# Causal attention with a soft mixture of experts: v loaded head by head

## Chip, cores and metric

The kernel runs on one core of one Trainium2 chip. The metric is the device time of one execution in microseconds (us). A profile of one execution, taken on the same kernel, gives the time of every instruction and DMA packet.

## What is computed

Attention over 8 batches and 8 heads, 576 queries, 16 "beacon" keys ahead of 576 causal ones, head size 64, all in float32; then a soft mixture of 8 experts with 4 slots each over the 4608 tokens of width 512.

```
k_all = concat([beacon_k, k]); v_all = concat([beacon_v, v])        # (B, H, 592, 64)
scores = q @ k_all.T / sqrt(64); causal mask past the beacons
a = softmax(scores)
x = (a @ v_all) laid out as (4608, 512)
logits = x @ phi                                                     # (4608, 32)
slot_input = softmax over tokens (logits).T @ x                      # (32, 512)
slot_out[e] = relu(slot_input[e] @ w1[e]) @ w2[e]                    # w1 (512, 1024), w2 (1024, 512)
out = softmax over slots (logits) @ slot_out                         # (4608, 512)
```

v has the shape (8, 8, 576, 64): the rows of one batch and one head lie in one piece, 64 float32 (256 B) a row, and the next head begins 147 KB further on.

## The kernel before

The kernel works through 32 pairs of heads, four pairs to a batch (the loop of line 571; n is the pair, b its batch, g its place in the batch). In each turn of the loop the program interleaves, in an order written out by hand for all engines (`manual_schedule`, line 531):

- `scores` (line 416): TensorE (PE) multiplies k and q in four pieces (L422), ScalarE (ACT) takes the exponential out of PSUM (L426), GpSimd (POOL) sets the masked part to zero (L434).
- `transposes` (line 395) of the next pair's q and k on PE (L404), copied out by VectorE (DVE; L409, L413).
- `attend` (line 439): PE multiplies the exponentials of the pair before by v (L448); `normalize` divides on DVE (L459 to L462).
- `x_transposes`, `logits`, `dispatch` and `combine_T` for a batch that is done.
- `cast_v` (line 360): POOL turns v of the next batch from float32 into float16, in five chunks of up to 128 rows. Chunks 0 to 2 are cast at the end of the first pair of a batch, chunks 3 and 4 at the end of the second. The 16 beacon rows are the first rows of chunk 0.
- `load_weights(2)` (line 380): POOL asks for two chunks of expert weights, 256 KB each as float16 (the transfer casts from float32), on a DMA queue of POOL's own, q0 in the profile.

The transfers of q, k, v and the beacons are asked for by SyncE (SP), on queue q1 in the profile. Their order on SP is that of the program. In the steady part, in the second pair of batch b, it asks for the first half of k and q of batch b+2 (L346), then for v of batch b+2 (the beacon rows, L352, then the five chunks, L356); in the fourth pair for the second half of k and q of batch b+2. So a round on SP is: two halves of k and q, four transfers of 576 KB; the beacon rows, 32 KB; five transfers of v, 224, 256, 256, 256 and 160 KB.

q and k have buffers for four halves each (pool `stq`, line 327). The float32 stage of v, `vstag`, has one buffer (pool `stv`, line 328, `bufs=1`): v of a batch can only be asked for when the last cast of the batch before it is done. The float16 copies, `vh`, are two.

The scheduler gives each transfer that SP asks for one of eight completion counters, in turn. A transfer therefore waits, on SP, until the transfer eight places before it on that queue has landed.

At the start SP asks for four transfers of k and q, eight for the beacon keys (32 KB each, L535), v of batch 0, two transfers of k and q, the router matrix phi (64 KB), two of k and q, v of batch 1 and two of k and q. After the last pair the experts are computed (L648 and following), and the output is written in 12 transfers (L717). A fallback path (`general_path`) for extreme inputs is not taken.

Of the kernel before, what the change touches and what calls it, by code (L numbers as in the profile page):

```python
# [268 lines left out]
def kernel(  # L269
# [12 lines left out]
    nc = tc.nc  # L282
    P = 128
    B, H, S, D = q.shape
# [51 lines left out]
    def head(g, hh):  # L336

        return 4 * (g // 2) + 2 * hh + g % 2
# [11 lines left out]
    def load_v(b):  # L350
        t = st["v", b] = stv.tile([P, NC5, H, D], FP, name="vstag", tag="v")
        nc.sync.dma_start(out=t[0:Nb, 0, :, :], in_=beacon_v[b].rearrange("h p d -> p h d"))  # L352
        lo = 0
        for c in range(NC5):
            p0, p1 = (Nb if c == 0 else 0), KW[c]
            nc.sync.dma_start(out=t[p0:p1, c, :, :],  # L356
                              in_=v[b, :, lo:lo + p1 - p0, :].rearrange("h p d -> p h d"))
            lo += p1 - p0

    def cast_v(b, c):  # L360
# [170 lines left out]
    with tc.manual_schedule(engines={ET.PE, ET.DVE, ET.Activation, ET.Pool, ET.SP}):  # L531
        bkf = stv.tile([P, H, D], FP, name="bkf", tag="bkf")
        load_qk(0, 0, first=True)
        for b in range(B):
            nc.sync.dma_start(out=bkf[Nb * b:Nb * b + Nb, :, :],  # L535
                              in_=beacon_k[b].rearrange("h n d -> n h d"))
        load_v(0)
        load_qk(0, 1)
        phif = work.tile([P, NDC, NSL], FP, name="phif", tag="phif", bufs=1)
        nc.sync.dma_start(out=phif[:, :, :], in_=moe_phi.rearrange("(c p) e -> p c e", p=P))  # L540
        load_qk(1, 0)
        load_v(1)
        load_qk(1, 1)

# [13 lines left out]
        for g in range(NG):  # L558
            nc.vector.tensor_copy(
                out=bkh[:, g, :, :],  # L560
                in_=bkf[:, head(g, 0):head(g, 1) + 1:2, :].bitcast(BF)[:, :, 1::2])
# [9 lines left out]
        for n in range(NPAIR + 4):  # L571
            b, g = divmod(n, NG)
# [30 lines left out]
            if live:  # L603
                if b + 1 < B and g < 2:
                    for c in ((0, 1, 2), (3, 4))[g]:
                        cast_v(b + 1, c)
                if g == 1 and b + 2 < B:
                    load_qk(b + 2, 0)
                    load_v(b + 2)
                if g == 3 and b + 2 < B:  # L610
                    load_qk(b + 2, 1)
                if n == NPAIR - 1:
                    siz = work.tile([P, NDC, E * (NSL + SPE)], F16, name="siz", tag="vc", bufs=1)
                    nc.gpsimd.memset(siz[:, :, :], 0.0)
                load_weights(2)
# [7 lines left out]
            out=siz[:, :, :].rearrange("p t (e w) -> p t e w", w=NSL + SPE)[:, :, :, 0:SPE],  # L623
# [56 lines left out]
        for src, w, low in ((stat, NST + 36 + NSL, SUM_LO), (so1, Dm, -SUM_HI)):  # L680
            lo = gd.tile([P, w], FP, name="lo", tag=f"lo{w}")
# [73 lines left out]
```

## Time and profile before

| what | us |
|---|---|
| median of three runs | 253.48 (251.63, 253.48, 261.88) |
| the profiled execution | 249.34 |
| its span, first to last instruction | 247.6 |
| busy: PE, DVE, ACT, POOL | 179.4, 125.2, 128.1, 121.7 |
| mean TensorE clock granted | 0.84 of full speed |
| issues of L356, 40 transfers of v: least, median, most | 0.424, 2.488, 7.911 |
| from an issue of a whole chunk of v (256 KB) to its landing, median | 11.0 |

How to read the profile: an engine's busy time is the time in its instructions. DMA share is the mean busy share of the core's 16 DMA engines; q0 is the queue of the weights, q1 that of everything SP asks for. The chain is followed back from the last instruction, at each step to what released it; "SPq L356" in it is SP issuing a transfer of line 356, "DMA vstag<-in_v_dram" is such a transfer under way. An issue on SP takes long where it waits for a counter or where the queue is full.

### The profile page before, as it was taken

The page shows a single profiled execution, that of the slowest core. Times are in us where ns is not written, and L with a number is a line of the kernel's source. Part 1 is how long each engine was busy: PE and PEld are TensorE (multiplying, and loading weights), DVE is VectorE, ACT ScalarE, POOL GpSimd, SP SyncE. Part 2 cuts the span into 40 slices and gives each one's busy share as a digit, 9 for nine tenths or more (in the row PEclk, how much of TensorE's full clock was granted, in tenths as well). Part 3 has the DMA queues.
Part 4 walks back from the last instruction along what each step waited for, and adds up shares of the span by engine and source line. Part 5 has one row for each costly group of instructions (what it writes and reads, how often), then busy time and mean ns, then how long its engine had stood idle before and what let it go on. Part 6 is the DMA issues. An engine that isn't in the chain of part 4 may idle for free.

```text
span 247.6 us, 8090 instructions
## 1 busy us (share of the span) xinstructions
PE 179.4 (72%) x3469; PEld 125.8 (51%) x3469; DVE 125.2 (51%) x277; ACT 128.1 (52%) x175; POOL 121.7 (49%) x256
## 2 busy tenths in 40 slices
PE   0345799849887987998699788749989697964350
PEld 0223466536665764766467566536766572531110
DVE  0305455705674586556348756535565630256650
ACT  2053547725674566568466677535689212055440
POOL 3042785296459365844945595187467500092000
PEclk9999999975996599589759999775899955999555
DMA  6699999999999999999999999999667720049993
GB/s 209 129 286 282 258 309 219 189 296 273 228 219 326 242 228 283 287 214 228 322 253 225 227 289 238 224 268 208 106 106 124 123 43 0 3 182 416 413 388 143
DMA packets 60061, 55.73 MB, mean 225 GB/s; under 512 B 42096, under 2 KB 42096, under 8 KB 60016
## 3 DMA queue, kind: packets, MB, share of 16 engines
q1 hardware_dynamic: 50800, 38.35, 53.0%
q0 software_dynamic: 9216, 16.78, 37.4%
q8 instruction: 29, 0.48, 0.7%
q14 instruction: 16, 0.13, 0.2%
HBM read 62.46 MB, written 9.44 MB: 290 GB/s over the span
## 4 chain that ended last, share of the span: by engine, by line
DMA 37%; PE 20%; POOL 13%; SPq 12%; DVE 8%; ACT 4%; issue 3%; DVEq 0%; POOLq 0%; ACTq 0%
DMA vstag<-in_v_dram 28%; SPq L356 11%; DMA out_dram<-osb 6%; PE av L448 5%; POOL vh L361 5%; POOL expT L434 5%; PE sc L422 4%; PE hps L648 3%; DVE x L462 2%; DMA qstag<-in_q_dram 2%; PE rsps L662 2%; ACT expT L426 2%; ACT osb L710 2%; DVE kT L413 1%; PE trps L404 1%
## 5 line engine op out<-in xcount | busy, mean ns | idle before, releaser
L426 ACT ACTIVATE expT<-sc 128x992 f16<-128x992 f32 (+3 forms) x128 | 107.1, 864 | 77.7 <-PE sc L422 75.6
L434 POOL TENSOR_SCALAR_AFFINE_SELECT expT<-expT 128x224 f16<-128x224 f16 (+3 forms) x128 | 54.3, 445 | 50.5 <-ACT expT L426 49.7
L448 PE MATMUL av<-vh,expT 128*128 128x65 f16 (+1 forms) x960 | 52.4, 214 | 14.3 <-POOL expT L434 12.6
L422 PE MATMUL sc<-qT,kT 64*128 64x80 bf16 (+4 forms) x576 | 52.3, 279 | 8.2 <-DVE qT L409 6.1
L448 PEld LDWEIGHTS <-expT 128*128 128x128 f16 (+1 forms) x960 | 41.5, 110 | 31.1 <-POOL expT L434 18.0
L361 POOL CAST vh<-vstag 128x512 f16<-128x512 f32 (+1 forms) x40 | 23.9, 614 | 29.8 <-DMA vstag<-in_v_dram 24.0
L459 DVE TENSOR_SCALAR stat<-av 128x10 f32<-128x10 f32 x32 | 5.4, 169 | 60.5 <-PE av L448 60.5
L413 DVE COPY kT<-trps 128x576 bf16<-128x576 bf16 x32 | 24.1, 752 | 7.9 <-PE trps L404 7.8
L422 PEld LDWEIGHTS <-kT 64*128 64x128 bf16 x576 | 18.2, 102 | 17.9 <-DVE qT L409 5.4
L462 DVE TENSOR_TENSOR x<-av,r 128x640 f16<-128x640 f32 x32 | 26.4, 825 | 1.1
L409 DVE COPY qT<-trps 128x576 bf16<-128x576 bf16 x32 | 23.9, 746 | 0.0
L475 PE MATMUL xtps<-idh,x 128*128 128x128 f16 (+2 forms) x160 | 15.4, 237 | 8.7 <-DVE kT L413 7.3
L710 ACT ACTIVATE osb<-fps,rc 128x512 f32<-128x512 f32 x18 | 11.6, 688 | 15.8 <-PE fps L707 11.2
L404 PE MATMUL trps<-idb,qstag 64*64 64x64 bf16 x576 | 17.0, 207 | 3.0 <-DVE xT L479 2.8
L404 PEld LDWEIGHTS <-kstag 64*64 64x64 bf16 x576 | 13.7, 122 | 9.1 <-issue 8.9
L404 PE MATMUL trps<-idb,kstag 64*64 64x64 bf16 x576 | 17.6, 210 | 0.0
L404 PEld LDWEIGHTS <-qstag 64*64 64x64 bf16 x576 | 15.0, 123 | 3.7 <-issue 3.7
L713 DVE TENSOR_SCALAR osb<-fps,rc 128x512 f32<-128x512 f32 x18 | 12.9, 748 | 7.7 <-DMA out_dram<-osb 5.3
L475 PEld LDWEIGHTS <-x 128*128 128x128 f16 (+2 forms) x160 | 11.4, 107 | 10.6 <-issue 6.9
L707 PE MATMUL fps<-so,eT 128*128 128x512 f16 x36 | 11.8, 442 | 5.6 <-ACT osb L710 4.5
L479 DVE COPY xT<-xtps 128x576 f16<-128x576 f16 x32 | 14.3, 449 | 1.4 <-PE xtps L475 1.0
L386 POOL DMA_DIRECT2D w1h<-in_moe_w_dram x24 | 13.2, 553 | 0.0
(68 smaller groups left out, 141.0 us busy)
## 6 DMA issues: line engine op xcount, KB each, us to landing
out_dram<-osb SPq DMA_DIRECT2D x12, 768.0 KB, 4.2
kstag<-in_k_dram SPq DMA_DIRECT2D x15, 576.0 KB, 7.9
qstag<-in_q_dram SPq DMA_DIRECT2D x15, 576.0 KB, 7.5
vstag<-in_v_dram SPq DMA_DIRECT2D x24, 256.0 KB, 11.0
w1h<-in_moe_w_dram POOLq DMA_DIRECT2D x24, 256.0 KB, 8.5
w2h<-in_moe_w_dram POOLq DMA_DIRECT2D x24, 256.0 KB, 8.8
wt<-in_moe_w_dram POOLq DMA_DIRECT2D x16, 256.0 KB, 4.9
vstag<-in_v_dram SPq DMA_DIRECT2D x8, 224.0 KB, 13.1
```

The costliest lines, as they stand in the source:

```text
L356: nc.sync.dma_start(out=t[p0:p1, c, :, :], in_=v[b, :, lo:lo + p1 - p0, :].rearrange("h p d -> p h d"))
L361: nc.gpsimd.tensor_copy(out=vhs[b % 2][0:KW[c], c, :, 0:D], in_=st["v", b][0:KW[c], c, :, :])
L404: nc.tensor.transpose(tp[64 * hh:64 * hh + 64, j, :], hi, idb[lo:lo + 64, lo:lo + 64])
L409: nc.vector.tensor_copy(out=qTs[n][:, :].rearrange("p (s j) -> p s j", j=NJ), in_=src)
L413: nc.vector.tensor_copy(out=kT[:, Nb:Nb + S].rearrange("p (s j) -> p s j", j=NJ), in_=src)
L422: nc.tensor.matmul(sc[:, hh, col:col + qw], kTs[n % 2][po:po + D, c * P:(c + 1) * P], qTs[n][po:po + D, q0:q0 + qw], start=True, stop=True)
L426: nc.scalar.activation(ex[:, :, base:base + w], sc[:, :, 0:w], AF.Exp, scale=scale)
L434: nc.gpsimd.affine_select(out=ap, in_=ap, compare_op=AL.is_ge, fill=0.0, base=cbase, pattern=pat, channel_multiplier=-1)
L448: nc.tensor.matmul(av[:, i, :], exps[n % 2][0:KW[c], hh, o:o + P], vhs[b % 2][0:KW[c], c, h, :], start=(c == 0), stop=(c == i))
L462: nc.vector.tensor_tensor(out=xs[b][:, :, head(g, 0):head(g, 1) + 1:2, :].rearrange("p i h d -> p h i d"), in0=av[:, :, :, 0:D], in1=r[:, ...
L475: nc.tensor.transpose(tp[:, QLO[i]:QLO[i] + QW[i]], xs[b][0:QW[i], i, 2 * t:2 * t + 2, :].rearrange("p h d -> p (h d)"), idh[0:QW[i], 0:QW ...
L710: nc.scalar.activation(osb[:, j - j0, :], fp_[:, :], AF.Copy, scale=rc[:, bb, j:j + 1])
```

## The change

In `load_v`, each of the five chunks of a batch is asked for in eight transfers, one per head, in place of one for all heads. A transfer then has 112, 128 or 80 rows of 256 B that lie in one piece in DRAM (28, 32 or 20 KB), and puts one 256 B row into each partition. The 40 transfers of v become 320. The beacon rows, the casts and the order of all other instructions are as before; each cast waits for the eight transfers of its chunk.

```
@@ -353,8 +353,8 @@
         lo = 0
         for c in range(NC5):
             p0, p1 = (Nb if c == 0 else 0), KW[c]
-            nc.sync.dma_start(out=t[p0:p1, c, :, :],
-                              in_=v[b, :, lo:lo + p1 - p0, :].rearrange("h p d -> p h d"))
+            for h in range(H):
+                nc.sync.dma_start(out=t[p0:p1, c, h, :], in_=v[b, h, lo:lo + p1 - p0, :])
             lo += p1 - p0
```

More of the change, by code (lines that the diff above doesn't have):

```diff
@@ L355, in load_v @@
             p0, p1 = (Nb if c == 0 else 0), KW[c]
-            nc.sync.dma_start(out=t[p0:p1, c, :, :],
-                              in_=v[b, :, lo:lo + p1 - p0, :].rearrange("h p d -> p h d"))
+            for h in range(H):
+                nc.sync.dma_start(out=t[p0:p1, c, h, :], in_=v[b, h, lo:lo + p1 - p0, :])
             lo += p1 - p0
```

## Prediction

> **What bounds the kernel now**
>
> I read the page first (shares, slices, queues), then the chain of waits in order of time, the waits of POOL, the DMA queue's own timeline on SP, and last the DMA view of short windows.
>
> The page:
>
> ```profile
> span 247.6 us, 8090 instructions
> ...
> DMA  6699999999999999999999999999667720049993
> ...
> DMA packets 60061, 55.73 MB, mean 225 GB/s; under 512 B 42096, under 2 KB 42096, under 8 KB 60016
> ## 3 DMA queue, kind: packets, MB, share of 16 engines
> q1 hardware_dynamic: 50800, 38.35, 53.0%
> q0 software_dynamic: 9216, 16.78, 37.4%
> ...
> DMA 37%; PE 20%; POOL 13%; SPq 12%; DVE 8%; ACT 4%; issue 3%; DVEq 0%; POOLq 0%; ACTq 0%
> DMA vstag<-in_v_dram 28%; SPq L356 11%; DMA out_dram<-osb 6%; PE av L448 5%; POOL vh L361 5%; POOL expT L434 5%; PE sc L422 4%; PE hps L648 3%; DVE x L462 2%; DMA qstag<-in_q_dram 2%; PE rsps L662 2%; ACT expT L426 2%; ACT osb L710 2%; DVE kT L413 1%; PE trps L404 1%
> ```
>
> See: no engine passes 72%, the DMA engines are full from about 12 to 173 us, and the largest item of the chain is the transfer of v. Most packets are under 512 B: those of v are 256 B rows, and 8 x 576 x 8 = 36864 of the 42096 are theirs.
>
> One batch in the chain (start, length, what), and how long POOL's casts wait for v (total, times, longest):
>
> ```profile
> 50.65 0.62 POOL vh L361
> 51.27 1.02 POOL w1h L386 x2
> 52.29 1.62 POOL expT L434 x4
> 53.91 1.13 POOL vh L361 x2
> ...
> 55.05 0.33 SPq L352
> ...
> 55.43 0.42 SPq L356
> ...
> 55.90 5.62 SPq L356
> ...
> 61.57 11.58 DMA vstag<-in_v_dram
> ```
> ```profile
> POOL vh L361 <- DMA vstag<-in_v_dram: 24.0, 12, 5.5
> ```
>
> See: vstag has one buffer. The last two casts of a batch free it, SP then asks for the next batch's v, its third chunk lands at 73.2 us, and the casts follow. The beacon transfers of line 352 that open a round stand at 32.27, 55.05, 77.67, 100.30, 122.41 and 144.58 us: a round takes 22.5 us.
>
> Price of an issue on SP, and of small transfers (timeline of SP; then the line view of L535 with the fewest, median and most ns, and its landing times):
>
> ```profile
> 2.67 2.80 SPq L535 DMA_DIRECT2D bkf<-in_beacon_k_dram  x6
> ```
> ```profile
> L535 SPq DMA_DIRECT2D bkf<-in_beacon_k_dram x8: 311/430/432, 2.7 to 7.7; - x8
> ...
> DMA to landing us min/median/max: 1.7/4.1/5.2
> ```
>
> See: transfers of 32 KB, the size that v gets, issued back to back, take 0.43 us each and start 0.475 us apart.
>
> The two queues together, from 63 to 65 us (v and weights), and the first queue with q and k almost alone, 52.5 to 54.5 us:
>
> ```profile
> q0 software_dynamic: 201, 0.35, 93.3%
> q1 hardware_dynamic: 200, 0.06, 19.7%
> ```
> ```profile
> q1 hardware_dynamic: 375, 0.77, 100.9%
> ```
>
> See: where weights (q0) and v (q1) meet, they go packet for packet, 201 to 200, although a weight packet is 2 KB (0.933 x 32 us / 171 = 0.175 us) and one of v 0.031 us. So v crawls beside weights. Alone, q and k move at 0.77 MB / 2 us = 385 GB/s.
>
> **The change, part by part**
>
> **Bytes and packets of v: nothing gained.** A row of v still lands as 256 B in its partition, so the 36864 packets stay. That one transfer now lies in one piece in DRAM could only help if pieces were joined; the first four k and q transfers also lie in one piece, and their packets are still 2304 B rows. Even a gain would hide behind the issue, below: the eight packets per engine of a 32 KB transfer take 8 x 18 ns = 0.15 us (q1 from 70.5 to 72.5 us, v without weights: 1615 packets in 92.3% of 32 us), against 0.475 us to issue it. 280 more transfers add 280 x 16 completion writes, 9 ns each in the packet records: 2.5 us per engine over the run, hidden in the same way. The casts on POOL wait for eight counters in place of one or two; only the last cast of a round is on the path, some 0.1 us each, 1 us in all and left out.
>
> **Issues: 320 in place of 40.** The duration is not in the trace for the new shape (128 rows of 256 B). Bounds: 0.37 us apart (the beacon issue of 0.33 us, plus the 0.045 us gap) and 0.66 us (the eight issues of L535 over 5.29 us, waits included). I take 0.475 us, the back-to-back rows of the same 32 KB. A batch of v then costs SP 40 x 0.475 = 19 us; today its first batch took 4.22 us. On SP alone a round would be 45 issues, 21.4 us, just under 22.5.
>
> **But they don't run beside q and k.** In both builds each SP transfer takes one of eight completion counters in turn, and is held until the transfer eight before has landed. A round on SP is: four transfers of k and q, the beacon rows, 40 of v. After q and k only three of v go freely; the fourth to seventh wait for q and k to land one by one, the eighth for the beacon rows. So the stream of v really starts when the last q has landed. The round becomes a sum:
> - four transfers of k and q: 4 x 0.59 MB / 385 GB/s = 6.1 us;
> - start and landing round them: 1.7 us, the shortest landing of L535;
> - the remaining 33 of v and the next k: 34 x 0.475 = 16.2 us;
> - weights: two chunks per pair, eight per round, 2.10 MB at 0.35 MB / (0.933 x 2 us) = 188 GB/s, 11.2 us of all engines. Bounds: 0 (all between issues that SP makes anyway: beside an idle ring v needs only 0.15 of its 0.475 us) and 11.2 (nothing moves in q1 meanwhile). Beside q and k they add nearly in full: the four transfers took from 51.5 to 64.5 us in place of 6.1. Beside v, eight transfers in flight keep SP going 8 x 0.475 = 3.8 us, more than one burst of two chunks (2.8 us alone), but not two in a row. I take half, 5.6.
>
> Sum 29.6 us, against 22.5. Compute needs no more than today's round, so it waits: behind a cast that waits on POOL stand the weight transfers and the masks (L434) of the next pair, for which PE's products with v (L448) wait; behind v on SP stand q and k, asked for a batch ahead, which do not come late.
>
> **The start.** SP reaches the first v at 8.48 us, ends its 40 issues at 27.5 (12.7 today). The first casts, which ended at 19.2 us, end near 30. Then four transfers of q and k and the router matrix (6.1 + 0.4 + 1.7 us) hold the counters to 35.7; 34 issues to 51.9; landing 1.7 and cast 0.6: the second batch is cast at 54.2 us, against 32.3. So +21.9.
>
> **The rounds.** Six more batches of v, five rounds of 29.6 and a last one with only two of q and k (26.6): 54.2 + 148 + 26.6 = 228.8 us. Today the last cast ends at 167.7. From there on nothing differs; the tail of 80 us stays. So +61.1 us, and 249.3 (the profiled execution; span 247.6 and 1.7 around it) gives 310.4. The median shown is 253.5, 1.7% above that execution; I keep to the execution.
>
> **Rivals**
>
> *Weights stop v altogether.* For: 200 against 201 packets; a 32 KB transfer beside weights needs 8 x (0.175 + 0.031) = 1.65 us, so the eight in flight last long. Against: bursts are 2.8 us with pauses. At the full 11.2 us a round is 35.2: 54.2 + 176 + 32.2 = 262.4, 344 us in all. Half the weights with 0.66 us an issue gives a round of 35.8 and 361.
>
> *Cheap issue, or weights hidden.* At 0.37 us a round is 26.0 and the second batch is cast at 46.4: 46.4 + 130 + 23 = 199.4, so 281 us. With 0.475 and weights at nothing: round 24.0, 54.2 + 120 + 21 = 195.2, so 277. For it: the 0.33 us of a lone beacon issue. Against: back to back no row shows it.
>
> *Not slower: the issue follows the size of a transfer.* If an issue cost SP in proportion to its packets, 128 in place of 1024, 0.42 us would become 0.05, SP would be done in 2 us, and only the ring would count, with the same bytes: a round of 22.5 and about 250 us. It decides from an issue under some 0.26 us, where start and rounds give back the 61 us. Against: L535, with 128 packets, costs 0.43 us, a whole chunk of v 0.42. The Trainium skill (DMA: Bandwidth & Descriptors, Issuing engines are not separate DMA queues) says that the sequencer's time to initiate a DMA is usually small relative to the DMA itself; by it this rival would hold, with 250 us. The rows disagree at this size: 0.475 us to issue what the ring moves in 0.15, which gives 310.
>
> *The one piece is read as one.* If it were, v at the 385 GB/s of q and k in place of 229 (70.5 to 72.5 us) would spare 2.1 us a round, 15 us in all and 235 us; but only with the rival before it, and no packet supports it.
>
> **How the numbers follow**
>
> Forecast, a round of 27.5 to 32.5 us (298 to 328 us): 0.62. Cheap issue or hidden weights (277 to 298): 0.18. Weights in full (328 to 361): 0.13, above that 0.02. Not slower: 0.04, and faster 0.01. The likeliest is 310 us. The range 281 to 344 takes the ends of the two unknown costs and leaves out the not-slower cases, the lowest of the second and the upper half of the third, under 0.2 together. 2%, about 5 us, is what a measurement of this kernel can tell from no change: faster 0.01, same 0.04, slower 0.95.
>
> **What would show it**
>
> Issue: the line of v on SP with 320 instructions near 0.43 us where it doesn't wait. Rounds: the beacon issues of line 352 some 30 us apart, the third of them near 54 us. Serial order: in a round, q and k packets first, then v at 60 to 70 GB/s (32 KB per 0.475 us) with the DMA share well under full. Chain: SP's issue of v as the largest item. POOL's waits for v should grow from 24 us to some 80. Wrong if the issues are under 0.3 us apart, if v flows while q and k are under way, or if compute rather than v ends the rounds.

## The result, and the profile after

The changed kernel takes 342.8 us (median of four runs, 339.8 to 343.8) against 252.6 us: a ratio of 1.359, 95% interval 1.345 to 1.373. The forecast was 310 us in a range of 281 to 344. The direction held, and the mechanism in the main; the size is 1.2 us under the upper end of the range. The profiled execution took 342.68 us, with a span of 341.0.

From the page after:

```profile
span 341.0 us, 8508 instructions
...
DMA  5226528965795579558955795379737968302995
...
DMA packets 64544, 55.78 MB, mean 164 GB/s; under 512 B 46576, under 2 KB 46576, under 8 KB 64496
## 3 DMA queue, kind: packets, MB, share of 16 engines
q1 hardware_dynamic: 55280, 38.36, 37.7%
q0 software_dynamic: 9216, 16.78, 28.9%
...
DMA 41%; SPq 24%; PE 16%; POOL 5%; DVE 4%; issue 4%; ACT 2%; DVEq 0%; POOLq 0%; ACTq 0%
DMA vstag<-in_v_dram 30%; SPq L357 23%; PE av L448 4%; DMA out_dram<-osb 4%; DMA qstag<-in_q_dram 3%; PE sc L422 3%; DMA kstag<-in_k_dram 3%; POOL expT L434 2%; DMA vstag<-in_beacon_v_dram 2%; PE hps L648 2%; PE lgps L486 2%; PE trps L404 1%; PE rsps L662 1%; DVE x L462 1%; DVE osb L713 1%
```

See three things. The row of DMA slices, solid nines before, now swings between 3 and 9 in the rounds: the engines wait for requests. The packets under 512 B rose by 46576 - 42096 = 4480, which is 280 x 16 completion writes and nothing else; the rows of v are still 36864 packets of 256 B. And SP's queue, 12% of the chain before, is 24%; SP's issue of v alone is 23%, second to the transfers of v with 30%.

The line view of the changed line (fewest, median and most ns of an issue; then landing), and SP's waits (total, times, longest):

```profile
L357 SPq DMA_DIRECT2D vstag<-in_v_dram x320: 312/430/1491, 8.6 to 259.6; - x160
...
DMA to landing us min/median/max: 1.6/2.2/15.1
```
```profile
SPq L357 <- DMA vstag<-in_v_dram: 28.9, 31, 2.6
SPq L357 <- DMA qstag<-in_q_dram: 26.4, 12, 4.6
SPq L357 <- DMA kstag<-in_k_dram: 13.1, 8, 3.5
SPq L357 <- DMA vstag<-in_beacon_v_dram: 6.9, 6, 1.3
```

See: an issue costs the 0.43 us that the beacon keys showed before. Where SP does not issue v, it waits for a completion counter: 75.3 us in all, more than half of it for k, q and the beacon rows.

One round on SP, and a piece of the chain in it (start, length, what):

```profile
90.64 0.34 SPq L352 DMA_DIRECT2D vstag<-in_beacon_v_dram  x1
91.03 30.50 SPq L357 DMA_DIRECT2D vstag<-in_v_dram  x40
...
124.95 0.34 SPq L352 DMA_DIRECT2D vstag<-in_beacon_v_dram  x1
```
```profile
92.66 14.28 DMA vstag<-in_v_dram
...
106.96 0.33 SPq L357
...
107.33 0.43 SPq L357
...
113.02 1.77 DMA vstag<-in_v_dram
```

See: 40 issues last 30.5 us. The first few stand in the queue behind k and q and then crawl beside the weights, until 107 us; from there on SP issues without a break until 119.6 us, where the last two wait for v transfers that crawl beside the next weights. The beacon issues stand at 59.30, 90.64, 124.95, 158.34, 193.14 and 229.18 us, 34.0 us apart (22.5 before).

The queues in both states, from 99 to 103 us, then from 108 to 114 us:

```profile
q0 software_dynamic: 387, 0.71, 94.1%
q1 hardware_dynamic: 387, 0.11, 18.8%
```
```profile
DMA packets 1851, 0.42 MB, mean 70 GB/s; under 512 B 1851, under 2 KB 1851, under 8 KB 1851
```

See: beside weights, as many packets of v as of weights, as before. Without them v moves at 70 GB/s, 32 KB per 0.475 us, and its engines are busy 31.8% of the time: the pace is SP's.

Where the 93.4 us of span went: the second batch is cast at 59.3 us in place of 32.2 (+27.1); from there to the last cast, 203.1 us in place of 135.5 (+67.6); the rest takes 78.6 in place of 79.9 (-1.3).

### The profile page after: what moved, and what is told of

Read it like the earlier page. It is cut to its first block, busy times and chain, and to the rows that moved or that the text cites. A ratio compares the mean times of both kernels' runs of the same rounds, so it can differ in the third digit from the quotient of the medians.

```text
span 341.0 us, 8508 instructions
## 1 busy us (share of the span) xinstructions
PE 198.4 (58%) x3469; PEld 136.7 (40%) x3469; DVE 124.4 (36%) x277; ACT 128.6 (38%) x175; POOL 122.1 (36%) x256
## 2 busy tenths in 40 slices
DMA packets 64544, 55.78 MB, mean 164 GB/s; under 512 B 46576, under 2 KB 46576, under 8 KB 64496
## 4 chain that ended last, share of the span: by engine, by line
DMA 41%; SPq 24%; PE 16%; POOL 5%; DVE 4%; issue 4%; ACT 2%; DVEq 0%; POOLq 0%; ACTq 0%
DMA vstag<-in_v_dram 30%; SPq L357 23%; PE av L448 4%; DMA out_dram<-osb 4%; DMA qstag<-in_q_dram 3%; PE sc L422 3%; DMA kstag<-in_k_dram 3%; POOL expT L434 2%; DMA vstag<-in_beacon_v_dram 2%; PE hps L648 2%; PE lgps L486 2%; PE trps L404 1%; PE rsps L662 1%; DVE x L462 1%; DVE osb L713 1%
## 5 line engine op out<-in xcount | busy, mean ns | idle before, releaser
L448 PE MATMUL av<-vh,expT 128*128 128x65 f16 (+1 forms) x960 | 60.4, 225 | 78.2 <-POOL expT L434 77.3
L448 PEld LDWEIGHTS <-expT 128*128 128x128 f16 (+1 forms) x960 | 46.6, 117 | 99.8 <-POOL expT L434 87.8
L361 POOL CAST vh<-vstag 128x512 f16<-128x512 f32 (+1 forms) x40 | 24.6, 614 | 129.7 <-DMA vstag<-in_v_dram 126.3
L422 PE MATMUL sc<-qT,kT 64*128 64x80 bf16 (+4 forms) x576 | 56.5, 302 | 21.8 <-DVE qT L409 20.3
L422 PEld LDWEIGHTS <-kT 64*128 64x128 bf16 x576 | 18.9, 108 | 32.3 <-DVE qT L409 19.6
L413 DVE COPY kT<-trps 128x576 bf16<-128x576 bf16 x32 | 24.1, 754 | 11.2 <-PE trps L404 11.1
L409 DVE COPY qT<-trps 128x576 bf16<-128x576 bf16 x32 | 23.9, 747 | 0.0
L475 PE MATMUL xtps<-idh,x 128*128 128x128 f16 (+2 forms) x160 | 17.0, 254 | 8.6 <-DVE kT L413 7.2
L404 PE MATMUL trps<-idb,qstag 64*64 64x64 bf16 x576 | 18.2, 215 | 2.5 <-DVE xT L479 2.4
L404 PEld LDWEIGHTS <-kstag 64*64 64x64 bf16 x576 | 14.8, 130 | 10.6 <-issue 7.0
L404 PE MATMUL trps<-idb,kstag 64*64 64x64 bf16 x576 | 18.7, 218 | 0.0
L404 PEld LDWEIGHTS <-qstag 64*64 64x64 bf16 x576 | 16.1, 131 | 3.1 <-issue 3.1
L475 PEld LDWEIGHTS <-x 128*128 128x128 f16 (+2 forms) x160 | 12.5, 115 | 10.8 <-issue 6.6
L707 PE MATMUL fps<-so,eT 128*128 128x512 f16 x36 | 13.0, 490 | 4.9 <-ACT osb L710 4.0
```

The costliest lines, as they stand in the source:

```text
L361: nc.gpsimd.tensor_copy(out=vhs[b % 2][0:KW[c], c, :, 0:D], in_=st["v", b][0:KW[c], c, :, :])
L404: nc.tensor.transpose(tp[64 * hh:64 * hh + 64, j, :], hi, idb[lo:lo + 64, lo:lo + 64])
L409: nc.vector.tensor_copy(out=qTs[n][:, :].rearrange("p (s j) -> p s j", j=NJ), in_=src)
L413: nc.vector.tensor_copy(out=kT[:, Nb:Nb + S].rearrange("p (s j) -> p s j", j=NJ), in_=src)
L422: nc.tensor.matmul(sc[:, hh, col:col + qw], kTs[n % 2][po:po + D, c * P:(c + 1) * P], qTs[n][po:po + D, q0:q0 + qw], start=True, stop=True)
L448: nc.tensor.matmul(av[:, i, :], exps[n % 2][0:KW[c], hh, o:o + P], vhs[b % 2][0:KW[c], c, h, :], start=(c == 0), stop=(c == i))
```

## Experiments

Times are device us; each batch ran beside the kernel before on the same chip (251.5, 252.2 and 252.0 us). Rounds are the distances of the beacon issues in the steady part. Runs given without an interval are single ones.

### Few weights, in the changed kernel and in the kernel before

```
-    wchunks = [(e, m, j) for es_ in ((0, 1, 2, 3), (4, 5)) for m in range(2)
-               for e in es_ for j in range(4)]
-    tail = [(e, m, j) for m in range(2) for e in (6, 7) for j in range(4)]
-    wchunks += tail
+    wchunks = [(e, m, j) for m in range(2) for e in (0, 1) for j in range(4)]
+    tail = []
...
     def weight(e, m, j):
...
+        e = e % 2
```

> The changed kernel with 16 of the 64 weight transfers: experts 2 to 7 use the weights of experts 0 and 1 (that part of the computation is left out). The weights then move in the first eight pairs alone, and the last four rounds have none. Theory (issues on SP and the eight completion counters set the round; the weights' time on the shared engines comes on top nearly in full): a round with weights stays near 32 to 34 us, one without falls to the sum of the other terms, 6.1 + 1.7 + 16.2 = 24.0 us; about 295 us in all. Rival (weights slow v only where SP would have waited anyway; the extra 4 us a round over the forecast come from the small transfers themselves): rounds stay at 30 us or more, total 320 to 340 us.

> The kernel before, with the same 16 of 64 weight transfers (experts 2 to 7 use the weights of experts 0 and 1). If the full DMA engines set its round of 22.5 us, rounds without weights fall to what compute needs, some 18 to 20 us, and the total to 230 to 240 us. If compute set it, the total stays at 249 us within 2%.

Measured: 316.7 us for the changed kernel, 229.7 for the kernel before. A round of the changed kernel in which no weight moves:

```profile
152.94 0.34 SPq L352 DMA_DIRECT2D vstag<-in_beacon_v_dram  x1
153.33 25.25 SPq L357 DMA_DIRECT2D vstag<-in_v_dram  x40
...
181.29 0.51 SPq L352 DMA_DIRECT2D vstag<-in_beacon_v_dram  x1
```

Such rounds last 28.7 us (124.32 to 210.49 in three), against 34.0 with weights: the weights cost 5.3 us a round, not their full 11.2. So the first theory was wrong in saying "nearly in full", and also in its 24.0 us for the rest; the total lies just under the 320 to 340 us of the rival, which had put the excess outside the weights. What is missing there shows in the DMA slices of this kernel from 151 to 162 us (0.275 us each), in which SP gets no more than the first eight of v issued:

```profile
DMA  1179559999999999999999999999720140030003
...
q8 instruction: 2, 0.03, 1.4%
```

The first k is asked for at 150.6 us, but the engines move at their full rate only from 152.7 on. The packets of k and q fill them to about 159 us, and the last q transfer lands at 160.8: the number of 2304 B packets per us falls from 166 (157 to 158 us) to 41, 7 and 1. A transfer has landed when its last completion write has come. Of the sixteen of this q, fifteen had come by 159.1 us; the last one came 1.6 us later. The eighth v transfer is issued 10.5 us after the first k, where the forecast had 7.8. In the four rounds of k, q and v without weights these are 10.0, 10.5, 11.2 and 10.6 us, though the late last write stands out in two of them only.

Two of the 33 issues from the eighth v on last 1.3 and 1.4 us without a wait that the profile names, 1.9 us more than their share. From its first k to the next this round takes 10.5 + 33 x 0.475 + 1.9 = 28.1 us; the forecast's 24.0 has 7.8, one issue more and no long ones.

In the kernel before, rounds without weights fall from 22.5 to 17.8 us (96.73 to 132.30 in two): there the full engines had set the round.

### Issue alone

The same few weights, and no k and q transfers after the first two batches.

```
-        t = st["kq"[which], b, hb]
+        t = st["kq"[which], b % 2, hb]
...
-                    load_qk(b + 2, 0)
                     load_v(b + 2)
-                if g == 3 and b + 2 < B:
-                    load_qk(b + 2, 1)
```

> The changed kernel with 16 of the 64 weight transfers (experts 2 to 7 use the weights of experts 0 and 1) and without the k and q transfers of batches 2 to 7 (they use k and q of batches 0 and 1); both parts of the computation are left out. In the later rounds SP then asks for v and the beacon rows alone, on engines that are nearly idle. Theory (the price of an issue on SP is the floor): round 40 x 0.475 = 19.0 + 0.4 for the beacon rows + 3.5 from the last issue to its landing, the cast and the next beacon issue = 22.9 us, as long as a whole round of the kernel before; about 280 us in all, against 316.7 with k and q. Rival (the issues hide; what costs is waiting on k, q and weights): rounds of 18 us or less, as compute had them in the kernel before with few weights, and about 255 us.

Measured: 289.0 us; the late rounds are 24.6 us (111.97 to 185.88 in three).

```profile
160.78 0.32 SPq L352 DMA_DIRECT2D vstag<-in_beacon_v_dram  x1
161.15 22.53 SPq L357 DMA_DIRECT2D vstag<-in_v_dram  x40
185.88 0.32 SPq L352 DMA_DIRECT2D vstag<-in_beacon_v_dram  x1
```

With the engines nearly idle, a round with v alone takes longer than a whole round of the kernel before (22.5 us). The 40 issues are 20.9 to 22.5 us of it; landing, cast and the next beacon issue are the rest. The theory's floor stands; it was 1.7 us too low, since it had 19 us for the issues.

### Tiny extra transfers, v not divided

The kernel before, with seven transfers of 2 KB behind each of v's 40.

```
+    dum = stv.tile([Nb, 7, D // 2], FP, name="dum", tag="dum")
...
+            for i in range(7):
+                nc.sync.dma_start(out=dum[:, i, :], in_=beacon_v[b, i, :, 0:D // 2])
```

> The kernel before, v in 40 transfers of all heads, and after each of them seven transfers of 2 KB (16 rows of 128 B) to a scratch tile that nobody reads: as many issues on SP and as many completion counters taken as in the changed kernel, but v not divided. Theory (issues and counters): rounds of 31 to 35 us, total 325 to 345 us. Rival (the division of v itself costs, by its pieces on the engines): about 250 to 260 us.

Measured: 360.5 us, rounds of 36.5 (95.16 to 241.02 in four). As many requests with hardly a byte in the extra ones cost more than the change; a 2 KB transfer also takes 0.42 us to issue in the median. The number of requests is enough for a loss of this size; the division of v's data is not needed for it. But the round is not made in quite the same way: in each steady round one issue, that of the first extra transfer behind k, q, the beacon rows and a whole chunk, lasts 9.1 to 10.1 us without a wait that the profile names, where the changed kernel waits for counters. Each chunk also waits for the chunk before it, eight places ahead, but only 8.5 us in the whole run. What makes the excess over the changed kernel was not tried apart.

### Two and four heads per transfer

```
-            for h in range(H):
-                nc.sync.dma_start(out=t[p0:p1, c, h, :], in_=v[b, h, lo:lo + p1 - p0, :])
+            for h in range(0, H, 2):
+                nc.sync.dma_start(out=t[p0:p1, c, h:h + 2, :],
+                                  in_=v[b, h:h + 2, lo:lo + p1 - p0, :].rearrange("h p d -> p h d"))
```

and the same with 4 for 2.

> v asked for in 160 transfers of two heads each. Theory (number of issues on SP, and the eight counters): round 6.1 + 1.7 + 14 x 0.475 + about 10 of weights = 24.5 us, second batch cast near 41 us, 41 + 5 x 24.5 + 21.5 = 185 against 167.7: about 266 us. Rival (cost grows evenly from 40 to 320 transfers): 40 to 320 gave +91 us, so 160 gives +39, 288 us. Rival (the loss is in transfers that lie in one piece of one head): back at 250 us.

> v asked for in 80 transfers of four heads each. Theory (issues and counters cost only what exceeds the engines' time): ten issues a round, 11.9 for k, q and beacon rows to land + 4 x 0.475 + 5.5 of weights = 19.3 us, under the 22.5 that the engines need, so as the kernel before: 246 to 258 us. Rival (the cost grows evenly with the number of transfers, 91 us for 280 more): 265 us.

| transfers of v | us (median) | ratio to before, 95% interval | round, us |
|---|---|---|---|
| 40 | 252.0 | | 22.5 |
| 80 | 257.9 | 1.020 (1.012 to 1.028) | 23.6 |
| 160 | 277.3 | 1.107 (1.094 to 1.120) | 26.1 |
| 320 | 342.8 | 1.359 (1.345 to 1.373) | 34.0 |

The first 40 extra transfers add 1.1 us to a round, the next 80 add 2.5, the last 160 add 7.9: little while SP works behind full engines, then 0.39 us for each of the last 20 of a round, nearly the price of an issue. 160 came out between the two expectations (266 and 288). That the terms that were short above are short here too is likely, but was not taken apart. 80 came out 2% slower, at the upper end of the 246 to 258 us expected, where the theory had seen no loss. Each ratio is to the kernel before in its own batch.

### k and q between the chunks of v

In the changed kernel, then in the kernel before.

```
...
                 if g == 1 and b + 2 < B:
-                    load_qk(b + 2, 0)
-                    load_v(b + 2)
+                    load_v(b + 2, (0,))
+                    load_qk(b + 2, 0, which=(0,))
+                    load_v(b + 2, (1,))
+                    load_qk(b + 2, 0, which=(1,))
+                    load_v(b + 2, (2,))
                 if g == 3 and b + 2 < B:
-                    load_qk(b + 2, 1)
+                    load_qk(b + 2, 1, which=(0,))
+                    load_v(b + 2, (3,))
+                    load_qk(b + 2, 1, which=(1,))
+                    load_v(b + 2, (4,))
```

> The changed kernel with the four k and q transfers of a round asked for singly between the chunks of v, one after each eight v transfers, in place of all four ahead of v; nothing else moved. Theory (the wait for k and q on the eight counters is serial to v's issues): it is now covered by the issues between; round 45 x 0.475 = 21.4, 3.3 for landing and cast, 5 for weights, about 30 us in place of 34: 312 to 325 us in all. Rival (the number of issues alone, or the amount moved, sets the round): 335 to 345 us.

> The kernel before with the same order: one k or q transfer after each of the first four chunks of v. Theory (full DMA engines set the round of 22.5 us, in any order): 245 to 256 us; slower than 256 if the engines run dry between the landing of the last chunk and the cast that frees the buffer, since no k and q are queued there any more; a gain over 5 us would say that v's place behind k and q, and not the engines, set the round.

Measured: 334.4 us (ratio to before 1.340, 1.316 to 1.364), below every run of the changed kernel itself (331.2 to 338.4 against 339.8 to 343.8, on another chip), but a gain of 8 us and not of 18 to 31. That is next to the rival's 335 to 345 us and far from the theory's 312 to 325, and the intervals of the two ratios overlap. The gain shows in the rounds, 34.0 us in the changed kernel: they are 32.3 us here (59.13 to 220.74 in five). SP's waits show where the rest went:

```profile
SPq L360 <- DMA vstag<-in_v_dram: 26.0, 35, 1.5
SPq L360 <- DMA kstag<-in_k_dram: 14.4, 13, 3.1
SPq L353 <- DMA vstag<-in_v_dram: 9.5, 11, 2.3
SPq L360 <- DMA qstag<-in_q_dram: 8.2, 8, 2.2
SPq L353 <- POOL vh L363: 4.2, 6, 0.8
```

L360 waits 48.6 us for counters in place of 75.3. But now nothing is queued between the last v and the beacon rows, and L353, the beacon issue, waits for landing and cast, 13.7 us, where it had k and q to issue before. In part a wait was traded for another.

The kernel before in this order: 257.1 us, ratio 1.040 (1.024 to 1.055), rounds of 23.9. Its engines run dry in the same gap: from 79.65 to 81.0 us, between the beacon issue and the next k, queue q1 keeps them busy for 2.2% of the time.

### Two buffers for the stage of v

The changed kernel with few weights, and `bufs=2` for the pool of vstag. Here only the weights of two experts have buffers of their own (`NRES = 2` in place of 6); `bkf` keeps one buffer.

> The changed kernel with 16 of the 64 weight transfers (experts 2 to 7 use the weights of experts 0 and 1), as in the run with few weights, which took 316.7 us with rounds of 28.3 us where no weights move; and vstag with two buffers in place of one. Theory (SP's queue is in order; the serial part is the wait of the fourth to eighth v transfer for k, q and the beacon rows): the cast that frees the buffer is not what SP waits for, rounds stay at 28 us, total 310 to 320 us. Rival (the single buffer makes the round serial): v is asked for a round earlier, rounds near 22 us, total under 295 us.

Measured: 311.5 us, against 316.7 with one buffer (single runs, on two chips); rounds without weights 28.1 us (123.04 to 207.29 in three), against 28.7. The single buffer, on which the chain before ran, is not what makes the round of the changed kernel.

### Not in one piece

The changed kernel, each transfer reading rows at least 1 KB apart; these are not the rows that the computation needs.

```
-                nc.sync.dma_start(out=t[p0:p1, c, h, :], in_=v[b, h, lo:lo + p1 - p0, :])
+                nc.sync.dma_start(out=t[p0:p1, c, h, :], in_=v[b, h, c:c + 4 * (p1 - p0):4, :] if c < 4 else
+                                  v[b, h, 0:7 * (p1 - p0):7, :])
```

> The changed kernel with the same 320 transfers, each reading rows that are 1 KB or more apart in DRAM (every fourth row of the head, every seventh for the last chunk; the rows of v are therefore wrong for the computation), so that no transfer lies in one piece. Theory (packets of 256 B either way, issue and counters set the round): 336 to 349 us, as the changed kernel. Rival (one piece in DRAM moves faster, and that gain is in the changed kernel already): over 349 us.

Measured: 340.4 us (338.4 to 342.1), against 342.8, on different chips; the ratio to before is 1.375 (1.355 to 1.396), and its interval overlaps that of the change. Lying in one piece in DRAM buys nothing here.

## Why the prediction was right, and by how much not

**Bytes and packets.** Right: the only new packets on SP's queue are 4480 completion writes, and the run with rows apart is as fast.

**Issues.** Right: 0.43 us, 0.475 apart, the row of the beacon keys. That price for 32 KB, not in proportion to packets, decided the sign; the not-slower rival is out. The sentence of the Trainium skill (DMA: Bandwidth & Descriptors, Issuing engines are not separate DMA queues) that the time to initiate a DMA is usually small relative to the DMA does not hold at this size if the DMA is its packets: 0.475 us against 31.8% of it, 0.15 us, the share in which v kept the engines busy when SP alone set the pace. Against its landing, 2.2 us in the median, an issue is still small; but landings overlap, and issues on one queue do not. Some issues of 0.6 to 1.5 us had no place in the sum: 1.9 us in the round that was taken apart, some 0.7 us a round in the changed kernel. Four of 1.3 to 1.5 us in the changed kernel begin within 0.4 us of a 16 KB packet of an instruction queue. The kernel before has as many packets on that queue, 29; whether fetching instructions is the cause was not tried.

**Not beside k and q.** Right in kind: 46.4 us of counter waits are for k, q and the beacon rows. As the forecast round put it, *start and landing* were 1.7 us, "the shortest landing of L535". That is the term that was mis-sized: without weights the eighth v came 10.0 to 11.2 us after the first k and not 7.8, and in the round taken apart start and landing make 4.4 us. The shortest landing of a 32 KB transfer on idle engines covers neither the 2.1 us from the first request until the engines move at their full rate nor a late last completion write. No run changed the number of counters, so how much of these waits more of them would spare is not shown.

**Weights.** The half taken, 5.6 us, was measured as 5.3, the difference of the rounds with and without them. That the half fits so closely is luck: it was a choice between the bounds 0 and 11.2. Some three fifths of it lie before the eighth v of a round (14.0 us after the first k, against 10.6 without weights), the rest behind it. I thought the weights mis-sized when I saw 34.0 us; the run with few weights refuted that.

**The sum.** Without weights the forecast round was 24.0 us and was measured as 28.7, 4.7 more; the weights gave back 0.3. Five rounds lost 4.4 us each, 22 us of the 32.3 that were missing. In the round taken apart the term for start and landing is 2.7 us short and the long issues are 1.9; the shares differ from round to round. The last round was miscounted: four transfers of k and q stand ahead of the last v too, the two that I left out come after it, and it lasts 33.2 us in place of 26.6 (6.6 more). The start gave 5.1: the second batch is cast at 59.3 and not 54.2 us. Its 40 issues end at 54.7 in place of 51.9, and its last v lands 4.2 us after its issue, beside the first weights, where the sum had 1.7. The rest of the kernel gave back 1.3.

That 342.8 us still lies in the range is partly luck as well. The upper end, 344, stood for weights in full, which did not come; nearly all the terms that were off were too small, and together they filled that room.

**Signs to look for.** The v stream at 60 to 70 GB/s (70 measured), the engines under full (31.8%), SP's issues of 0.43 us: seen. SP's issue of v was to be the largest item of the chain and is the second, 23% behind the 30% of the transfers of v. The third beacon issue came at 59.3 us and not near 54. POOL's wait for v was to be some 80 us and is 126.3; each of the five casts of a batch now waits for its own chunk, 37 times against 12.

## What to carry to other kernels

Before dividing a transfer, multiply the number of requests of a round by the price of one issue on its queue, taken from back-to-back rows of the trace, and compare it with the round; here 45 x 0.475 = 21.4 us already matched it, and the waits that could not be covered came on top. Ask what each request must wait for in an in-order queue with a fixed number in flight: small transfers behind large ones use up the places and stop. Here a piece that lies together in DRAM was no gain, since it landed as short rows; look at the packets, not at the address pattern.

## What the runs showed of the hardware that was not expected

The last of several large transfers can wait for a single completion write. In the round taken apart fifteen of the last q's sixteen came by 159.1 us and the last at 160.8; from 159.4 to 159.6 us one packet was under way where some sixteen had been before. A 16 KB packet of an instruction queue had begun at 156.5 us and taken 1.08 us. In the next round one began at 182.8 us, and the last write of the last q came 2.0 us after the fifteenth; in the round after that, with no such packet among k and q, it came 0.5 us after it. But in the first round without weights it came 0.4 us after it in spite of such a packet at 129.6 us. So an instruction packet may be what holds one engine up; this is not shown.

And the granted TensorE clock was lower in the slower kernel, 0.738 against 0.840 in the profiled executions (0.68 to 0.738 in all four runs of the changed kernel), though the same 3469 matmuls left PE idle more of the time; they were busy 198.4 us in place of 179.4. In the kernel before with few weights it was 0.872. PE is 16% of the chain here, and the reason was not looked for.
